# Decode step of two attention + feed-forward layers: stationary gate and up weights, group two's queries behind half of group one's scores, norm sums on the adds, value steps in other places

## The chip, the cores and the metric

The kernel runs on one core of a Trainium2 chip. The time is the device time of one execution in microseconds (us). A run more than 1.5% above the fastest run of the same kernel is marked "slow" and stays out of the ratios. A ratio is the mean time of one kernel's fast runs over that of the kernel before in the same rounds on the same chip, so it is not quite the ratio of the medians that stand beside it.

## The reference, cut to what matters

```python
x = x + attention(layernorm(x), k_cache, v_cache, wq, wo)   # layer one
x = x + ffn(layernorm(x), w_gate, w_up, w_down)
x = x + attention(layernorm(x), k_cache, v_cache, wq, wo)   # layer two: the same caches and weights
x = x + ffn(layernorm(x), w_gate, w_up, w_down)
# x: 4 x 1 x 512 bf16; 32 query heads, 8 key/value heads, 4096 positions, 128 per head
# ffn(x) = (gelu(x @ w_gate) * (x @ w_up)) @ w_down, inner width 1792
```

The two caches are 67 MB, which would be 134 MB if each layer read them. The kernel keeps a batch's keys on the chip for its second layer and loads values twice, less a few tiles that it keeps. With the weights it moves 110.4 MB.

## The kernel before

One pass per batch b: the dense part of b's first layer, then the second layer's attention of b **interleaved** with the first layer's attention of b+1. Second-layer scores read key tiles that are still on the chip; each group of four tiles is then overwritten by keys of b+1 (`keys.load`). VectorE turns every key tile once it has landed (`turn`, 1.22 us each in the mean). A **value step** is 16 matmuls on one value tile of 0.5 MB. It takes a loaded buffer, frees one, and so lets a further value load be issued. After every fourth step VectorE normalises the result. Everything is hand-scheduled. VectorE takes its work in program order in the traces: before, it sat idle for 1.84 us ahead of a normalisation at 217.47 us, and the query transpose behind that, whose rows were done at 216.92, started at 217.89. All large loads go through one queue (q1, 110.38 MB). In the trace of before, the 146 of them whose landing it tells landed in the order of their issue, tiles asked for in a row some 1.28 us apart (key tiles at 242.63, 243.91 and 245.23).

```python
def load_v():                                   # value loads; blocked while keys have the queue
    while not seen["hold"] and free and seen["load"] < seen["upto"]:
        ...
        dq.dma_start(out=v[:], in_=cache_tile(A_v_cache, b, g * GH + s, t))

def step(self, count=1):                        # a value step
    ...
    load_v()
    for i in range(CH):
        nc.tensor.matmul(self.ot[:, s % 2], lhsT=v[:, i, :], rhs=pe[:, s, c, :], ...)
    free.append(held.pop((b, g, s, t)))
    load_v()
    if self.n % (2 * NT) == 0:                  # every fourth: normalise on VectorE
        nc.vector.tensor_tensor(out=self.dst(...), in0=self.ot[:], in1=rden[:, s0:s0 + 2], op=ALU.mult)

def ffn_in(b0, nb, w_sb):                       # gate or up: activations stationary, weights moving
    for k in range(KD):
        for j in range(QD):
            nc.tensor.matmul(rows[...], lhsT=xn_bf[:, k, bs], rhs=w[:, j], ...)   # 448 columns
    return rows                                 # turned by VectorE later

def dense(b0, nb, proj, fill):
    out_proj_end(*proj)                         # T0 of the text: its first matmul
    add_y(b0, nb, y); ln_square(b0, nb)
    fill(1)                                     # fill = value steps left of the second layer
    mv = ln_center(b0, nb)
    fill(1)
    rg = ffn_in(b0, nb, wg_sb)
    sq, h = gelu(nb, rg, ln_rstd(nb, mv))       # ln_rstd: ten small VectorE operations
    fill(1)
    ru = ffn_in(b0, nb, wu_sb)
    H_bf = gate_up(nb, sq, h, ru)
    fill(3)
    y = down(nb, H_bf)
    add_y(b0, nb, y)

# between dense(b) and the next attention
    ln_square(b, 1); fill(1); mv = ln_center(b, 1); fill(1)
    rstd = ln_rstd(1, mv); am = ...             # reciprocal root of the second norm
    qr0 = q_rows(b, 1, ga); fill(1)
    qm0 = q_spread(turn_rows(qr0, 512)[:, :, 0], am, ga)
    qr1 = q_rows(b, 1, gb); fill(1)             # both groups' queries before any score
    q_build(qm0, ga); qm1 = q_spread(turn_rows(qr1, 512)[:, :, 0], am, gb)

# attend(): start of the interleaved attention
    for t in range(NT):
        scores(sc2[0], ga, t); keys.load(GH)    # four key tiles free: four loads
    last_q()                                    # q_build(qm1, gb)
    seen["hold"] = True                         # no value loads from here
    rest(2)                                     # rest = fill
    for t in range(NT):
        scores(sc2[1], gb, t); keys.load(GH)
    rest(1); seen["hold"] = False; load_v()
    p0 = soft(sc2[0]); rest(1); ...
    qm = q_spread(q1_bf[:, ga, :, b1], amask, ga)
    turn()                                      # key turn 1
    q_build(qm, ga); vals2.step(KEEP); turn(3)  # key turns 2 to 4
```

## Time and profile before

| | before |
|---|---|
| median of the runs beside the first run of the changed kernel | 324.09 us (321.3 to 324.54) |
| span of the profiled execution | 322.7 us |
| T0 of batch 0, 1, 2 and of the last pass | 135.13, 200.56, 266.49, 310.14 us |
| periods between them; T0 of the last pass to the end | 65.4, 65.9, 43.7; 12.6 us |
| value loads held up by TensorE's value steps | 70.8 us in 59 waits |
| VectorE turning keys | 75.9 us in 64 operations |

The lines that carry this are in the prediction. In all such lines the idle time in front of an instruction stands last, in square brackets, with what ended it. "x8" merges eight like instructions in a row, and the duration is then that of the whole row. L426, L446, L333, L340 and L351 are the value load, the value step, the key load, the key turn and the scores. In the changed kernel they are L446, L466, L351, L358 and L369.

### The profile page before, as it was taken

Reading aid. Unit: us, or ns where it says so; the run is one execution under the profiler, and the core shown is the slowest. Engines: PE = TensorE matmul, PEld = TensorE weight load, DVE = VectorE, ACT = ScalarE, POOL = GpSimd, SP = SyncE. Lnnn points to the kernel's source line nnn. Section 1 sums busy time; section 2 is a strip of 40 time slices with the busy share of each in tenths; the row PEclk is TensorE's granted clock in tenths of the full one; section 3 lists DMA queues with packets and bytes.
Section 4 is the critical chain, followed back from the end, with each engine's and each line's share of the span. In section 5 each row is a group of like instructions: output and inputs, shape, how many; then the busy total and the mean of one; then the engine's idle time right before and its main releaser. Section 6 shows DMA issues by size and latency. Waiting matters only on the chain.

```text
span 322.7 us, 8609 instructions
## 1 busy us (share of the span) xinstructions
PE 212.4 (66%) x3812; PEld 120.8 (37%) x3812; DVE 171.9 (53%) x459; ACT 28.9 (9%) x70; POOL 0.7 (0%) x6
## 2 busy tenths in 40 slices
PE   1460575334665369898663498989645889896864
PEld 0010244121322145663421256644202565546442
DVE  5576750033457895255497742543989435434133
ACT  0003010000020103000202021001010120012000
POOL 0000000000000000000000000000000000000000
PEclk9999999999996555556955555557655555577555
DMA  7999999999959998999899999998999999989900
GB/s 256 391 412 399 409 409 396 349 389 374 353 172 365 408 380 281 383 346 341 288 415 408 410 385 352 365 314 263 411 408 409 407 396 359 291 295 373 364 22 3
DMA packets 34646, 110.94 MB, mean 344 GB/s; under 512 B 3112, under 2 KB 9008, under 8 KB 34608
## 3 DMA queue, kind: packets, MB, share of 16 engines
q1 hardware_dynamic: 34608, 110.38, 92.0%
q8 instruction: 30, 0.49, 0.6%
q14 instruction: 8, 0.07, 0.1%
HBM read 110.37 MB, written 0.00 MB: 342 GB/s over the span
## 4 chain that ended last, share of the span: by engine, by line
DMA 57%; PE 25%; DVE 8%; SPq 6%; issue 2%; ACT 1%; ACTq 0%
DMA kt<-in_A_k_cache_dram 25%; DMA v<-in_A_v_cache_dram 23%; PE ot L446 6%; PE sc L351 6%; DMA wd_sb<-in_B_w_down_dram 5%; PE rows L209 4%; DMA kt<-in_A_v_cache_dram 3%; SPq L126 3%; DVE kt L340 2%; PE rows L264 2%; PE rows L285 2%; PE x L397 1%; PE y L270 1%; SPq L127 1%; DVE pp L378 1%
## 5 line engine op out<-in xcount | busy, mean ns | idle before, releaser
L340 DVE STREAM_TRANSPOSE kt<-kt 128x1024 f32<-128x1024 f32 x64 | 75.9, 1222 | 9.0 <-DMA kt<-in_A_k_cache_dram 8.4
L446 PEld LDWEIGHTS <-v 128*128 128x128 bf16 x1920 | 59.6, 104 | 54.9 <-DMA v<-in_A_v_cache_dram 31.0
L446 PE MATMUL ot<-pe,v 128*128 128x4 bf16 x1920 | 64.2, 166 | 23.4 <-DMA v<-in_A_v_cache_dram 19.6
L351 PE MATMUL sc<-kt,qb 128*32 128x512 bf16 x512 | 62.0, 534 | 19.3 <-DVE kt L340 16.6
L351 PEld LDWEIGHTS <-qb 128*32 128x32 bf16 x512 | 16.9, 113 | 49.5 <-issue 26.3
L199 DVE STREAM_TRANSPOSE rows<-rows 128x512 f32<-128x512 f32 (+1 forms) x25 | 17.6, 702 | 29.0 <-PE rows L264 15.3
L453 DVE TENSOR_TENSOR OT_bf<-ot,rden 128x8 bf16<-128x8 f32 x32 | 5.5, 171 | 40.4 <-PE ot L446 38.0
L370 ACT ACTIVATE pp<-sc,nm 128x512 bf16<-128x512 f32 x16 | 11.0, 688 | 158.1 <-DVE junk L366 126.8
L397 PE MATMUL x<-pp,ident_bf 128*32 128x128 bf16 x256 | 9.1, 283 | 24.1 <-DVE pp L378 23.9
L209 PE MATMUL rows<-wq_sb,xn_bf 128*1 128x512 bf16 (+1 forms) x160 | 18.6, 620 | 5.0 <-DMA wq_sb<-in_A_wq_dram 4.5
L264 PE MATMUL rows<-wo_sb,OT_bf 128*1 128x512 bf16 (+1 forms) x120 | 14.8, 614 | 6.6 <-DMA wo_sb<-in_A_wo_dram 6.4
L397 PEld LDWEIGHTS <-ident_bf 128*32 128x32 bf16 x256 | 6.7, 121 | 30.2 <-issue 28.1
L357 DVE TENSOR_REDUCE m<-sc 128x1 f32<-128x512 f32 x16 | 10.8, 673 | 12.1 <-PE sc L351 12.1
L378 DVE STREAM_TRANSPOSE pp<-pp 128x512 bf16<-128x512 bf16 x16 | 11.2, 702 | 5.6 <-ACT pp L370 5.2
L233 DVE TENSOR_TENSOR qb<-qe,amask 128x256 bf16<-128x256 f32 x16 | 6.8, 424 | 11.8 <-PE qe L230 11.8
L400 ACT CAST pe<-x 128x512 bf16<-128x512 f32 x16 | 9.4, 585 | 21.9 <-PE x L397 21.9
L315 PE MATMUL y<-H_bf,wd_sb 128*128 128x1 bf16 (+1 forms) x280 | 8.3, 165 | 3.9 <-DVE H_bf L308 2.3
L285 PE MATMUL rows<-wu_sb,xn_bf 128*1 128x448 bf16 (+1 forms) x80 | 8.4, 570 | 2.9 <-DMA wu_sb<-in_B_w_up_dram 2.9
L285 PE MATMUL rows<-wg_sb,xn_bf 128*1 128x448 bf16 (+1 forms) x80 | 8.3, 567 | 2.9 <-DMA wg_sb<-in_B_w_gate_dram 2.4
L315 PEld LDWEIGHTS <-wd_sb 128*128 128x128 bf16 x280 | 7.9, 104 | 5.6 <-DMA wd_sb<-in_B_w_down_dram 3.5
L276 DVE TENSOR_TENSOR XX<-XX,y 128x4 f32<-128x4 f32 (+1 forms) x10 | 1.6, 161 | 15.6 <-PE y L315 9.2
L383 PE MATMUL den<-zx,mean_f 128*128 128x16 f32 x32 | 8.9, 357 | 0.0
(66 smaller groups left out, 117.4 us busy)
## 6 DMA issues: line engine op xcount, KB each, us to landing
v<-in_A_v_cache_dram SPq DMA_DIRECT2D x112, 512.0 KB, 8.1
kt<-in_A_k_cache_dram SPq DMA_DIRECT2D x64, 512.0 KB, 10.6
wq_sb<-in_A_wq_dram SPq DMA_DIRECT2D x2, 2048.0 KB, 11.1
wo_sb<-in_A_wo_dram SPq DMA_DIRECT2D x4, 1024.0 KB, 12.0
kt<-in_A_v_cache_dram SPq DMA_DIRECT2D x8, 512.0 KB, 9.9
wg_sb<-in_B_w_gate_dram SPq DMA_DIRECT2D x1, 1792.0 KB, 13.4
wu_sb<-in_B_w_up_dram SPq DMA_DIRECT2D x1, 1792.0 KB
wd_sb<-in_B_w_down_dram SPq DMA_DIRECT2D x2, 896.0 KB, 16.6
```

Of the source, the lines that this page charges most:

```text
L199: nc.vector.transpose(out=rows[:, :n], in_=rows[:, :n])
L209: nc.tensor.matmul(rows[j * QS:j * QS + nb, :], lhsT=xn_bf[:, k, bs], rhs=w, start=(k == 0), stop=(k == KD - 1))
L264: nc.tensor.matmul(rows[r0:r0 + lhsT.shape[-1], :], lhsT=lhsT, rhs=wo_sb[:, i, :], start=(at == 0 and n < QD), stop=(at == 2 and n >= hp - ...
L285: nc.tensor.matmul(rows[j * QS:j * QS + nb, :KF * QS], lhsT=xn_bf[:, k, bs], rhs=w[:, j], start=(k == 0), stop=(k == KD - 1))
L315: nc.tensor.matmul(y[:, k], lhsT=wd_sb[:, c, k * P:(k + 1) * P], rhs=H_bf[:, c, :], start=(c == 0 and k == 0), stop=(c == KF - 1), skip_gr ...
L340: nc.vector.transpose(out=words, in_=words)
L351: nc.tensor.matmul(sc[s * QS:(s + 1) * QS], lhsT=qb[:, w0:w0 + 2 * W], rhs=kt[:, :, be // 2, :, be % 2], start=(t == 0 and be == 0), stop= ...
L357: nc.vector.tensor_reduce(out=m[:], in_=sc.rearrange("p c j -> p (c j)"), axis=AX.X, op=ALU.max)
L370: nc.scalar.activation(out=pp[:], in_=sc[:], func=ACT.Exp, bias=nm[:, 0:1], scale=scale, accum_out=ls[:])
L378: nc.vector.transpose(out=flat, in_=flat)
L397: nc.tensor.matmul(x[a * QS:(a + 1) * QS, s], lhsT=ident_bf[:, s * QS:(s + 1) * QS], rhs=pT[:, a], start=True, stop=True, skip_group_check ...
L446: nc.tensor.matmul(self.ot[:, s % 2], lhsT=v[:, i, :], rhs=pe[:, s, c, :], start=(c == 0), stop=(c == C - 1), skip_group_check=True)
```

## The change

The change means to bring the first key loads forward and to keep TensorE busy in its gaps. Its parts are:

- gate and up weights become the stationary operand, which spares two transposes per dense part;
- the queries of head group two are built only after half of group one's scores, whose keys are then free earlier;
- the sums for the norm come from accumulators of the adds;
- value steps move from the dense part into later gaps, and second-layer values alone may be loaded while keys have the queue.

```diff
     def ffn_in(b0, nb, w_sb):
-        for k in range(KD):
-            for j in range(QD):
-                nc.tensor.matmul(rows[...], lhsT=xn_bf[:, k, bs], rhs=w[:, j], ...)
+        for c in range(KF):
+            for k in range(KD):
+                nc.tensor.matmul(h[:, c], lhsT=w_sb[:, k, c * P:(c + 1) * P], rhs=xn_bf[:, k, bs], ...)
 ...
     def load_v():
-        while not seen["hold"] and free and seen["load"] < seen["upto"]:
-            b, g, s, t = loads[seen["load"]]
+        while free and seen["load"] < seen["upto"]:
+            b, last, g, s, t = loads[seen["load"]]
+            if seen["hold"] and not last:
+                return
 ...  attend()
-            for t in range(NT):
-                scores(sc2[0], ga, t)
-                keys.load(GH)
-            last_q()
             seen["hold"] = True
-            rest(2)
+            scores(sc2[0], ga, 0)
+            keys.load(GH)
+            qm1 = next_q()
+            scores(sc2[0], ga, 1)
+            keys.load(GH)
+            q_build(qm1, gb)
+            rest(1)
             for t in range(NT):
                 scores(sc2[1], gb, t)
                 keys.load(GH)
-            rest(1)
             seen["hold"] = False
             load_v()
             p0 = soft(sc2[0])
-            rest(1)
+            rest(2)
             soft_turn(p0)
             pe0, den0 = soft_swap(p0, p2p), soft_den(p0)
+            rest(2)
             qm = q_spread(q1_bf[:, ga, :, b1], amask, ga)
             turn()
             prob2[ga] = (pe0, soft_recip(den0))
             q_build(qm, ga)
+            rest(1)
             vals2.step(KEEP)
             turn(3)
 ...  dense()
+        fill(1)
         add_y(b0, nb, y)
         ln_square(b0, nb)
-        fill(1)
         mv = ln_center(b0, nb)
         fill(1)
         rg = ffn_in(b0, nb, wg_sb)
-        rstd = ln_rstd(nb, mv)
-        sq, h = gelu(nb, rg, rstd)
+        ru = ffn_in(b0, nb, wu_sb)
         fill(1)
-        ru = ffn_in(b0, nb, wu_sb)
-        H_bf = gate_up(nb, sq, h, ru)
-        fill(3)
-        y = down(nb, H_bf)
+        sq, h = gelu(nb, rg, ln_rstd(nb, mv))
+        y = down(nb, gate_up(nb, sq, h, ru))
+        fill(1)
 ...  between dense() and attend()
         ln_square(b, 1)
-        fill(1)
         mv = ln_center(b, 1)
         fill(1)
+        qr0 = q_rows(b, 1, ga)
+        fill(2)
         rstd = ln_rstd(1, mv)
         am = ...
-        qr0 = q_rows(b, 1, ga)
+        q_build(q_spread(turn_rows(qr0, 512)[:, :, 0], am, ga), ga)
         fill(1)
-        qm0 = q_spread(turn_rows(qr0, 512)[:, :, 0], am, ga)
-        qr1 = q_rows(b, 1, gb)
-        fill(1)
-        q_build(qm0, ga)
-        qm1 = q_spread(turn_rows(qr1, 512)[:, :, 0], am, gb)
+        def next_q():
+            return q_spread(turn_rows(q_rows(b, 1, gb), 512)[:, :, 0], am, gb)
```

The norm sums (`accum_out` on the add and on the square), the last batch's steps and one probability buffer less are left out here.

## The prediction

> **What bounds the kernel now.** I read the page first: busy shares, the DMA queue, the chain that ended last.

> ```profile
> PE 212.4 (66%) x3812; PEld 120.8 (37%) x3812; DVE 171.9 (53%) x459; ACT 28.9 (9%) x70; POOL 0.7 (0%) x6
> ...
> q1 hardware_dynamic: 34608, 110.38, 92.0%
> ...
> DMA 57%; PE 25%; DVE 8%; SPq 6%; issue 2%; ACT 1%; ACTq 0%
> ```

> No engine is near full; the DMA queue is, and the chain runs through it for 57%. At the best sustained rate in the page's slices, about 409 GB/s, 110.38 MB would take 270 us. The span is 322.7. The end holds 13.4 us without transfers (last value tile lands at 309.3), the start about 3; some 36 us are lost in between. Then the waits of the DMA queue's own engine, to see what transfers wait for:

> ```profile
> SPq L426 <- PE ot L446: 70.8, 59, 4.8
> ...
> SPq L333 <- PE sc L351: 18.3, 8, 11.5
> ```

> Value loads (L426) wait for value steps on TensorE to free a buffer, key loads (L333) for scores to free a key tile. The table by stretches shows where the rate falls:

> ```profile
> 206.00:218.00 12.00, 10.62 (x219) 6.36 (x211) 5.81 (x29) 0.22 (x1) 0.00 (x0) 0.50 0.95 324
> 218.00:224.00 6.00, 5.97 (x93) 2.73 (x97) 2.45 (x8) 0.35 (x1) 0.00 (x0) 0.65 0.86 271
> ...
> 235.00:245.00 10.00, 4.71 (x50) 2.00 (x49) 8.64 (x15) 1.67 (x4) 0.00 (x0) 0.50 1.03 410
> ```

> The last column is GB/s. The dense part and the first scores (206 to 224) run below 409; the key stretch runs full. From 200 to 226 the one-microsecond stretches miss 6.15 us of transfer. That is what the change aims at, once in each of the batch turns. The timeline of VectorE in the same turn shows the other chain, the turning of keys:

> ```profile
> 217.47 0.18 DVE L453 TENSOR_TENSOR OT_bf<-ot,rden 128x8 bf16<-128x8 f32 x1 [1.84 <-PE ot L446]
> ...
> 226.61 1.25 DVE L340 STREAM_TRANSPOSE kt<-kt 128x1024 f32<-128x1024 f32 x1 [0.16 <-DMA kt<-in_A_k_cache_dram]
> ...
> 228.62 10.16 DVE L340 STREAM_TRANSPOSE kt<-kt 128x1024 f32<-128x1024 f32 x8
> ```

> Eight turns take 10.16 us, 1.27 each, which is the landing rate of a key tile (0.524 MB at 410 GB/s is 1.28); five with tiles at hand take 5.74 (1.15 each). VectorE turns keys as they land and is nearly saturated doing so.

> [...]the normalisation of values at 217.47 sits 1.84 us for its TensorE step, and the query work behind it stays behind. [...]In the trace tiles of one queue land one after another, 1.28 us apart. [...]

> **The change part by part.** I compare the two programs' instruction order, and count time from T0, the first matmul of the closing output projection (135.13, 200.56 and 266.49; periods 65.4 and 65.9).

> *Gate and up stationary.* 16 matmuls of 448 columns (1.66 us per pass) become 56 of one column. The down projection already has that form: 56 in 1.63 to 1.67. TensorE: no change. VectorE loses two transposes of 0.66 per dense pass. In the last pass, where nothing fills, the first one stands on the chain (314.59, 0.61), and up is done before it is wanted: about -0.7 us with its gap, at the end.

> *Norm sums on the adds.* Twice per batch a reduction (0.17 + 0.03) leaves the chain, two accumulator reads of about 0.08 enter it (the row of L366 shows 0.08): -0.05 each. Nothing.

> *Dense and query chain.* After: gate and up back to back from T0+2.6 to 5.9, one step, down from 6.4 to 8.1 (before 8.1 to 9.7), mean by 9.4, query rows 9.8 to 11.7. But two value steps now stand before the reciprocal root in program order, and the first ends a head pair. Its normalisation on VectorE waits for a TensorE step that stands behind the query rows: 12.2. Only then come ten operations of 0.19 and the mask (to 14.5), transpose 0.76, spread 0.24, qe 0.25, qb 0.45: first scores at about T0+16.3. Before: 16.6, 17.5 and 17.3. [...]I give the scores the half clock (16 in 1.85): first key tiles free at about 18.0, against 17.7 in the first full period (152.86-135.13) and 19.4 in the second (219.95-200.56). So the intended lead of 4 us shrinks to -0.3 to +1.4.

> *Group two's queries after half the scores.* The second four key tiles free 1.8 + 1.8 us later, near 21.6. Four tiles in flight cover that (4 x 1.28). Scores of the second group shift from 22.0 to about 22.6.

> *Value steps moved behind the scores.* This is the part I distrust. Before, 10 of 14 remaining value steps ran ahead of the key loads, so all 14 tiles were requested first. After, 8 do. The fourteenth tile is requested by the ninth step, so in the queue it stands behind eight key tiles. Its step now stands on TensorE before the new scores, and its normalisation on VectorE between key turn 1 and key turn 2. So turns 2 to 8, which overlapped the landing of keys 2 to 8, start only after all eight keys and one value tile have landed.
> Landing: if the queue kept 1.28 per tile from tile 13 (T0+19.3): 19.3 + 9 x 1.28 = 30.8. Before, the eighth key landed 15 to 16 us after the first key's issue because the rate sags there (271 GB/s above): 18.0 + 15.5 + 1.28 = 34.8. I take 33.3. Then step and normalisation 0.7: turn 2 at 34.0, against 26.5 (161.67) and 28.1 (228.62). From turn 2 to the end of turn 16 before: 250.56-228.62 = 21.9, less 0.8 because tiles are at hand: 21.1. So turn 16 ends at 55.1, and the second half of the last scores starts there. Before it started at 51.05 and 51.6, and was held by values: the step ahead waited for its tile, with keys ready 2.4 and 1.6 us earlier. From there to the next T0 are 14.4, less 0.4 as value tiles are now at hand. Period: 55.2 + 13.9 = 69.1, so +3.7 and +3.2 us.

> *First turn (batch 0 to 1), no value steps left over:* query chain 0.25 earlier, keys landing-bound: -0.2. *Last turn:* keys are not loaded, tile 14 takes the first freed buffer, unblocked. But three steps now precede the second softmax; its probabilities reach TensorE at T0+31.9 instead of 29.3. From there 11.7 us of work (14.04 less 2.34 of waits): 43.6 against 43.4. With the tail -0.7: -0.5.

> Sum: 323.9 - 0.2 + 3.7 + 3.2 - 0.5 = 330.1. I shade it to 329.0, because someone chose this order.

> **The rivals.** (1) *Transfers stay fed, and gain wins.* If the reciprocal root ran beside the query rows and tile 14 came early, each of three turns would return up to half of its 6 us: 315. For it: the queue's 92% and its 70.8 us of waits for TensorE. Against it: the two in-order waits, which the order shows. (2) *It cancels.* With ideal landing (30.8) the turns end at 52.6: +1.2 and +0.7, total 325. For it: 2 us of slack in front of the value waits. Against it: the sag at every start of key loads. (3) *The sag is full at each start* (34.8): +5 each, 333.[...]

> **Range and chances.** The doubt is the landing of tile 14, 4 us wide and counted twice, hence 8 us between rivals 2 and 3, plus my reading of order. Range 321 to 336. Two per cent slower begins at 330.4, just above my estimate: 0.40. Two per cent faster (317.4) needs rival 1: 0.08. Between: 0.52.

> **What would show it.** Right: in the VectorE timeline of turns two and three, the first key turn, then a value normalisation with an idle time of several us ended by TensorE, that TensorE step in turn waiting for a value transfer, then seven key turns at 1.15; the value transfer issued after eight key loads; periods near 69. In the dense part ten small operations starting only after a normalisation near T0+12. In the tail no transpose, about 0.7 less. Wrong: no idle before turn 2, or tile 14 landed before T0+29, or periods under 65.

## The result, and the profile after

The changed kernel took 339.11 us (336.6 to 341.95, 4 runs, one of them slow) against 324.09 before: ratio 1.0456, 95% interval 1.0345 to 1.0568. It is slower by 4.6%, above the predicted range. The changed kernel was run once more as it stood. The lines below are from it. Its span is 340.5. The execution took 342.32 us and is the slowest of its four (median 339.77), so its periods add up to some 2 us more than is usual.

The page's busy shares, DMA queue and chain, of the changed kernel:

```profile
PE 212.5 (62%) x4212; PEld 132.0 (39%) x4212; DVE 164.8 (48%) x465; ACT 29.1 (9%) x70; POOL 0.7 (0%) x6
...
q1 hardware_dynamic: 34608, 110.38, 87.9%
...
DMA 36%; PE 31%; DVE 21%; SPq 5%; issue 4%; ACT 1%; DVEq 0%; ACTq 0%
```

TensorE is as busy as before, VectorE less by 7 us, the bytes are the same. The queue's share fell from 92.0 to 87.9%, and the chain runs through VectorE for 21% in place of 8%. Only the weight loads got more work (PEld 132.0 us in place of 120.8), and they overlap the matmuls: from 230 to 238 us 3.98 us of loads and 7.39 of matmuls lie in 8.00. The rest got later. The waits of the DMA queue's engine agree: value loads wait longer for value steps.

```profile
SPq L446 <- PE ot L466: 100.0, 59, 5.0
...
SPq L351 <- PE sc L369: 17.0, 7, 11.7
```

The periods show where. T0 lies at 135.40, 209.31, 283.14 and 328.70:

| from T0 to the next | before | predicted | after (repeat) |
|---|---|---|---|
| first turn, start to T0 of batch 0 | 135.1 | 134.9 | 135.4 |
| batch 0 to 1 | 65.4 | 69.1 | 73.9 |
| batch 1 to 2 | 65.9 | 69.1 | 73.8 |
| batch 2 to the last pass | 43.7 | 43.6 to 43.9 | 45.6 |
| last T0 to the end | 12.6 | 11.9 | 11.8 |

The third row, in the DMA queue's timeline (when loads were issued; the duration is that of issuing all of them):

```profile
229.72 5.46 SPq L351 DMA_DIRECT2D kt<-in_A_k_cache_dram  x8
236.88 0.33 SPq L446 DMA_DIRECT2D v<-in_A_v_cache_dram  x1
238.16 9.26 SPq L351 DMA_DIRECT2D kt<-in_A_k_cache_dram  x8
```

One value tile, the fourteenth of its batch, stands behind eight key tiles. Before, sixteen key loads stood in one row, with all values asked for ahead of them:

```profile
219.95 16.68 SPq L333 DMA_DIRECT2D kt<-in_A_k_cache_dram  x16
```

TensorE's and VectorE's timelines of the changed kernel show what the new order does:

```profile
247.08 1.44 PE L466 MATMUL ot<-pe,v 128*128 128x4 bf16 x48 [8.50 <-DMA v<-in_A_v_cache_dram]
```

```profile
236.96 1.23 DVE L358 STREAM_TRANSPOSE kt<-kt 128x1024 f32<-128x1024 f32 x1
...
247.71 0.18 DVE L473 TENSOR_TENSOR OT_bf<-ot,rden 128x8 bf16<-128x8 f32 x1 [8.67 <-PE ot L466]
247.79 9.12 DVE L358 STREAM_TRANSPOSE kt<-kt 128x1024 f32<-128x1024 f32 x8
```

TensorE idles 8.50 us for that tile, and VectorE 8.67 us for TensorE, between key turn 1 and key turn 2. Seven of the eight keys that it then turns stood ahead of that value tile in the queue. This is the picture that was predicted, though the idle is longer. In the stretches of this time the transfers move 276, then 413 GB/s (columns: length, busy us of PE, weight load, VectorE, ScalarE and GpSimd with their counts, granted clock, DMA share, GB/s):

```profile
230.00:238.00 8.00, 7.39 (x150) 3.98 (x143) 4.46 (x12) 1.67 (x4) 0.00 (x0) 0.84 0.85 276
238.00:247.00 9.00, 0.58 (x20) 0.41 (x17) 0.76 (x3) 0.00 (x0) 0.00 (x0) 0.57 1.03 413
```

From 238 to 247 the queue moves 413 GB/s, and VectorE works 0.76 of 9 us while key tiles that have landed stand unturned: the eight turns that then follow take 9.12 us without a wait for a transfer. What VectorE leaves undone here it has to do later in the period.

The change was to feed the transfers better. The bytes moved in the 28 us after each T0 (summed from stretches of 4 us) say that it did the reverse:

| MB in the 28 us after T0 | batch 0 | batch 1 |
|---|---|---|
| before | 9.4 | 9.0 |
| after (repeat) | 8.1 | 7.2 |

The second in-order wait is in the query chain, on VectorE:

```profile
223.86 0.18 DVE L473 TENSOR_TENSOR OT_bf<-ot,rden 128x8 bf16<-128x8 f32 x1 [2.46 <-PE ot L466]
223.94 0.15 DVE L184 TENSOR_TENSOR msq<-mv 128x1 f32<-128x1 f32 x1
...
225.87 0.23 DVE L661 TENSOR_SCALAR am<-amask,rstd 128x4 f32<-128x4 f32 x1
```

The ten operations of the reciprocal root need nothing but sums that were copied at 221.25. They start 2.7 us after that, because a value normalisation ahead of them waits for its value step, which stands behind the query rows. TensorE then waits 2.80 us for the queries, which VectorE multiplies by the mask made from that root.

A third wait was not in the prediction. TensorE's timeline in the dense part of batch 1:

```profile
219.02 0.94 PE L333 MATMUL y<-H_bf,wd_sb 128*128 128x1 bf16 x30 [2.37 <-issue]
```

"issue" is idle time in which the engine waited for nothing that the profile shows. Each dense part with value steps in it has such idles, 2.1 to 2.9 us in all. More on them below.

Three causes are thus on the table: **A**, tile 14 behind the keys; **B**, the normalisation ahead of the reciprocal root; **C**, the stationary gate and up with their idle. They can be undone one at a time.

### The profile page after: what moved, and what is told of

Its sections match the earlier page's. It is cut to its first block, busy times and chain, and to the rows that moved or that the text cites.

```text
span 340.2 us, 9425 instructions
## 1 busy us (share of the span) xinstructions
PE 212.3 (62%) x4212; PEld 132.2 (39%) x4212; DVE 164.8 (48%) x465; ACT 29.2 (9%) x70; POOL 0.7 (0%) x6
## 2 busy tenths in 40 slices
DMA packets 34649, 110.99 MB, mean 326 GB/s; under 512 B 3112, under 2 KB 9008, under 8 KB 34608
## 3 DMA queue, kind: packets, MB, share of 16 engines
q1 hardware_dynamic: 34608, 110.38, 88.0%
## 4 chain that ended last, share of the span: by engine, by line
DMA 38%; PE 28%; DVE 21%; SPq 6%; issue 5%; ACT 1%; DVEq 0%; ACTq 0%
DMA v<-in_A_v_cache_dram 17%; DMA kt<-in_A_k_cache_dram 13%; DVE kt L358 11%; PE sc L369 7%; PE ot L466 6%; DMA wd_sb<-in_B_w_down_dram 5%; DMA kt<-in_A_v_cache_dram 3%; PE rows L224 3%; PE rows L304 3%; SPq L127 3%; PE y L333 2%; PE rows L279 2%; PE x L415 1%; DVE rows L214 1%; DVE m L375 1%
## 5 line engine op out<-in xcount | busy, mean ns | idle before, releaser
L466 PE MATMUL ot<-pe,v 128*128 128x4 bf16 x1904 | 63.1, 166 | 35.3 <-DMA v<-in_A_v_cache_dram 24.0
L358 DVE STREAM_TRANSPOSE kt<-kt 128x1024 f32<-128x1024 f32 x64 | 74.6, 1214 | 4.5 <-DMA kt<-in_A_k_cache_dram 4.4
L369 PE MATMUL sc<-kt,qb 128*32 128x512 bf16 x512 | 64.8, 543 | 15.7 <-DVE kt L358 12.8
L369 PEld LDWEIGHTS <-qb 128*32 128x32 bf16 x512 | 17.4, 114 | 47.3 <-issue 28.5
L214 DVE STREAM_TRANSPOSE rows<-rows 128x512 f32<-128x512 f32 x15 | 10.9, 730 | 34.8 <-PE rows L224 19.5
L375 DVE TENSOR_REDUCE m<-sc 128x1 f32<-128x512 f32 x16 | 10.9, 678 | 12.5 <-PE sc L369 12.5
L245 PE MATMUL qe<-qm,t_bf 128*128 128x64 bf16 x16 | 3.4, 213 | 14.9 <-DVE qm L235 14.1
L333 PE MATMUL y<-H_bf,wd_sb 128*128 128x1 bf16 (+1 forms) x280 | 8.5, 165 | 4.4 <-DMA wd_sb<-in_B_w_down_dram 2.7
L304 PE MATMUL rows<-xn_bf,wg_sb 128*128 128x1 bf16 (+1 forms) x280 | 8.3, 165 | 3.9 <-DMA wg_sb<-in_B_w_gate_dram 2.4
L304 PE MATMUL rows<-xn_bf,wu_sb 128*128 128x1 bf16 (+1 forms) x280 | 8.3, 165 | 3.7 <-DMA wu_sb<-in_B_w_up_dram 2.9
L292 DVE SCALAR_TENSOR_TENSOR XX<-XX,y 128x4 f32<-128x4 f32 x8 | 1.3, 158 | 18.9 <-PE y L333 13.6
L333 PEld LDWEIGHTS <-wd_sb 128*128 128x128 bf16 x280 | 8.1, 104 | 4.7 <-DMA wd_sb<-in_B_w_down_dram 2.9
L304 PEld LDWEIGHTS <-wg_sb 128*128 128x128 bf16 x280 | 8.2, 105 | 4.1 <-DMA wg_sb<-in_B_w_gate_dram 2.5
## 6 DMA issues: line engine op xcount, KB each, us to landing
wo_sb<-in_A_wo_dram SPq DMA_DIRECT2D x4, 1024.0 KB, 11.9
wd_sb<-in_B_w_down_dram SPq DMA_DIRECT2D x2, 896.0 KB, 16.8
```

Of the source, the lines that this page charges most:

```text
L214: nc.vector.transpose(out=rows[:, :n], in_=rows[:, :n])
L304: nc.tensor.matmul(h[:, c], lhsT=w_sb[:, k, c * P:(c + 1) * P], rhs=xn_bf[:, k, bs], start=(c == 0 and k == 0), stop=(k == KD - 1), skip_g ...
L333: nc.tensor.matmul(y[:, k], lhsT=wd_sb[:, c, k * P:(k + 1) * P], rhs=H_bf[:, c, :], start=(c == 0 and k == 0), stop=(c == KF - 1), skip_gr ...
L358: nc.vector.transpose(out=words, in_=words)
L369: nc.tensor.matmul(sc[s * QS:(s + 1) * QS], lhsT=qb[:, w0:w0 + 2 * W], rhs=kt[:, :, be // 2, :, be % 2], start=(t == 0 and be == 0), stop= ...
L375: nc.vector.tensor_reduce(out=m[:], in_=sc.rearrange("p c j -> p (c j)"), axis=AX.X, op=ALU.max)
```

## The experiments

All outputs are right. "Base" names the kernel that the diff is against.

**1. The changed kernel again** (4 runs).

> The changed kernel once more, for a profile in the fast state and an interval. Every theory expects 336 to 341 us and a period from one closing output projection to the next of about 73 us in the second and third batch (before: 65.4 and 65.9), with the value step before the new scores waiting about 8 us for its tile.

339.77 us, ratio 1.0492 (1.0427 to 1.0558). The result stands, and this run's profile is the one read above.

**2. A undone: one value step more ahead of the scores** (base: after).

```diff
         q_build(q_spread(turn_rows(qr0, 512)[:, :, 0], am, ga), ga)
-        fill(1)
+        fill(2)
 ...  attend(), attend_last()
         q_build(qm1, gb)
-        rest(1)
```

> The changed kernel with one value step moved from behind group two's queries to ahead of the first scores, so that the fourteenth value tile is requested before the eight keys instead of behind them. Theory A (that tile's wait holds VectorE between key turn 1 and 2): the wait of 8 us is gone in both periods, turn 8 ends some 7 us earlier, the value waits behind it take some of it back, periods near 67, time 325 to 329. Rival D (the key loads themselves come slowly because they now come in two bursts of four): the wait only changes its name, keys land as late, periods stay above 71, time 336 to 340.

328.44 us, ratio 1.0136 (1.007 to 1.0202): 11 of the 15 us come back. Periods are 66.0 and 67.3. The queue's timeline, then VectorE's, then TensorE's:

```profile
221.92 15.63 SPq L351 DMA_DIRECT2D kt<-in_A_k_cache_dram  x16
```

```profile
228.99 1.23 DVE L358 STREAM_TRANSPOSE kt<-kt 128x1024 f32<-128x1024 f32 x1
...
231.03 0.18 DVE L473 TENSOR_TENSOR OT_bf<-ot,rden 128x8 bf16<-128x8 f32 x1
231.11 9.12 DVE L358 STREAM_TRANSPOSE kt<-kt 128x1024 f32<-128x1024 f32 x8
```

```profile
249.06 0.59 PE L466 MATMUL ot<-pe,v 128*128 128x4 bf16 x16 [3.02 <-DMA v<-in_A_v_cache_dram]
```

All sixteen keys are asked for in one row. The normalisation waits for nothing, and eight turns run in 9.12 us right behind turn 1. In their place waits for value tiles return later in the period, 3.02 us here, so not all of the 8.67 us are gained. Rival D is out: the keys still come in two bursts of four, and the periods are well under 71.

**3. B undone: the reciprocal root ahead of the two value steps** (base: after).

```diff
         qr0 = q_rows(b, 1, ga)
-        fill(2)
         rstd = ln_rstd(1, mv)
         am = ...
+        fill(2)
```

> The changed kernel with the reciprocal root placed ahead of the two value steps in program order. Theory B (the normalisation in between makes the root wait for the query rows): first scores 2 us earlier in all three later batches; as the landing of tile 14 follows the first key request, both periods and the last batch shorten by about 2, time 332 to 335. If only A counts and the keys' landing is bound by transfers that are late anyway: under 1 us in all.

331.94 us, ratio 1.0235 (1.0182 to 1.0287). VectorE's timeline:

```profile
219.06 0.16 DVE L184 TENSOR_TENSOR msq<-mv 128x1 f32<-128x1 f32 x1
...
221.48 0.17 DVE L473 TENSOR_TENSOR OT_bf<-ot,rden 128x8 bf16<-128x8 f32 x1 [0.26 <-PE ot L466]
221.56 0.72 DVE L214 STREAM_TRANSPOSE rows<-rows 128x512 f32<-128x512 f32 x1
```

The ten operations follow the sums at once, and the normalisation waits 0.26 in place of 2.46. The periods are 70.9, 71.0 and 42.0, some 3 us shorter each than in the repeat, where 2 were expected.

**4. C undone: gate and up moving again** (base: after; `ffn_in`, `gelu` and `gate_up` of before).

> The changed kernel with gate and up computed as before (activations stationary, weights moving, 16 matmuls each, with the two transposes on VectorE). Theory C (with 56 pairs each, TensorE runs through its instructions faster than they are fetched, and stands idle 2.2 to 2.7 us per dense part with no wait on any engine): the unexplained idle of TensorE in the dense part is gone, two transposes of 0.66 are back and cost about 1.2, so each later batch gains 1.0 to 1.5, the tail loses 0.7: 335 to 337, 2 to 4 us under the changed kernel of these rounds. If the idle has another cause, it stays and the transposes cost: 341 to 343.

339.14 us, ratio 1.0466 (1.0415 to 1.0517), against 1.0492 for the changed kernel: 0.3%, within the intervals. That lies in neither of the two ranges that were expected. TensorE's timeline from the down projection of batch 1 on:

```profile
214.44 1.65 PE L335 MATMUL y<-H_bf,wd_sb 128*128 128x1 bf16 x56 [0.71 <-DVE H_bf L328]
215.95 0.57 PE L468 MATMUL ot<-pe,v 128*128 128x4 bf16 x16
```

The one idle, of 0.71 us, is for VectorE's product and not "issue". From 115 us on this run has one "issue" idle of 0.29 us on TensorE, in the last turn, and the kernel before has none. So the idles of the dense parts belong to the stationary form. In time, what they cost is, within the intervals, what the two transposes of 0.66 us cost that come back here. VectorE's timeline of this run, from the same turn, serves further down:

```profile
220.00 0.18 DVE L475 TENSOR_TENSOR OT_bf<-ot,rden 128x8 bf16<-128x8 f32 x1 [2.46 <-PE ot L468]
...
244.28 0.18 DVE L475 TENSOR_TENSOR OT_bf<-ot,rden 128x8 bf16<-128x8 f32 x1 [8.84 <-PE ot L468]
```

**5. A and B undone** (base: after).

> Both mended: fourteenth tile ahead of the keys, reciprocal root ahead of the value steps. tile14_first alone came to 1.014 of the kernel before and norm_early to 1.024 where the changed kernel has 1.049. If the two losses are separate and simply add (theories A and B), 1.014 less 0.025 is 0.99, 320 to 323 us. If they are two ways to the same loss (an earlier first score also brings tile 14 earlier, so norm_early bought part of A's wait), about 1.00 to 1.01, 324 to 328; then value transfers bound both, as they bound the kernel before.

322.92 us in 20 runs, ratio 0.9984 (0.9957 to 1.0011). Parity: A and B carry the whole loss. The time lies in the range expected if the two add, the ratio between the two expectations.

**6. A, B and C undone** (base: after).

> As tile14_norm, and gate and up with moving weights again. What is left of the change then: the split of the queries, the norm sums, fewer value steps ahead of the keys. Theory C (instruction fetch): TensorE's idle without a wait in the dense part goes, the transposes return, 1 us or so per later batch won, tail 0.5 to 0.7 lost: 0 to 3 us under tile14_norm. If transfers bound the periods by then, no difference but the tail, 0 to 1 us slower.

321.53 us (20 runs, three of them slow), ratio 0.9973 (0.9942 to 1.0004).

**7. Only the stationary gate and up** (base: before).

> The kernel before with gate and up stationary and nothing else of the change. Theory C: TensorE's idle without a wait appears here too, 1 to 3 us per dense part, at distances of 128 pairs; against it four transposes of 0.66 leave two chains, and the tail is 0.5 to 0.8 shorter: 322 to 326, no clear difference. If the idle came from the new order of steps instead, there is none here, and each dense part is over 1 us shorter: 319 to 322.

324.19 us, ratio 1.0002 (0.9961 to 1.0043). Its end is 0.8 us shorter (11.7), and it has 4.3 us of "issue" idle on TensorE in the dense parts, which eats what the transposes had cost there.

**8. Only the split of group two's queries** (base: before).

```diff
-            for t in range(NT):
-                scores(sc2[0], ga, t)
-                keys.load(GH)
-            last_q()
+            scores(sc2[0], ga, 0)
+            keys.load(GH)
+            qm1 = last_q()                    # rows, transpose and spread of group two
+            scores(sc2[0], ga, 1)
+            keys.load(GH)
+            q_build(qm1, gb)
```

> The kernel before with the second group's query rows between the two halves of the first scores, and nothing else. Theory A and B say the split itself is harmless: first keys requested 1.9 us earlier, the second four 1.8 later than they would be then, 322 to 325. Rival D (two bursts of four keys starve the queue, so the split costs): 327 or more, with a dip in the rate between the bursts.

320.79 us, ratio 0.9887 (0.9779 to 0.9995), with one of four runs slow: a gain, outside both expectations, but with too wide an interval.

**9. All three undone, A put back.**

> From all_three (0.997 of the kernel before), with only one step undone: one value step back behind group two's queries, so tile 14 is again requested behind eight keys. This is cause A alone. Theory A: the wait of 8 to 9 us returns, both periods grow from 64.7 to about 69 to 71 us, time 329 to 333. If A hurts only together with a late first score (B and C), the growth is under 2 us per period: 322 to 326.

331.30 us, ratio 1.0234 (1.0165 to 1.0303). Periods are 69.1 and 69.3, what the prediction had for the whole change.

**10. All three undone, B put back.**

> From all_three, with only the two value steps back ahead of the reciprocal root. Cause B alone. The first scores come about 2 us later in each of three batches; value transfers hide part of it in the two full periods, nothing hides it in the last batch: 324 to 328. If transfers hide it wholly in the full periods: 322 to 324.

327.55 us, ratio 1.0105 (1.0041 to 1.0169). With this the table of all eight combinations is full (each run against before on its own chip; three chips in all):

| | B absent | B present |
|---|---|---|
| A absent, C absent | 0.9973 | 1.0105 |
| A absent, C present | 0.9984 | 1.0136 |
| A present, C absent | 1.0234 | 1.0466 |
| A present, C present | 1.0235 | 1.0492 |

A costs 2.5 to 2.6% where B is absent and 3.6% where it is present. B costs 1.3 to 1.5% without A and 2.3 to 2.6% with it. C costs 0.0 to 0.3%. The interplay of 1% is no larger than its uncertainty: put together from the intervals, that of either half of the table is about 1.1%. A possible reason is that B makes the first key load late, and with A tile 14 stands behind those keys, so that the delay is passed on to all turns; this is not shown.

**11. The split alone again** (5 rounds).

> before_split once more with five rounds, as its first interval was 0.978 to 1.000. If the split alone gains (first keys requested earlier in three batches, 1 us each), 0.985 to 0.993; if the three fast runs were a lucky draw, 0.995 to 1.005.

319.49 us, ratio 0.9828 (0.9766 to 0.9891). Two of its six runs were slow and are left out, as are four of the 25 of before on that chip. The medians of all runs give 319.49 over 323.40, that is 0.988. The gain is clear of the noise, and lies near 1.1 to 1.7%.

**12. All three undone, the steps behind the query spread** (base: 6; two steps move behind the spread, and the last batch's second softmax ahead of its three steps).

> all_three with two more moves of the same kind: the two value steps go behind the query spread in program order, so no normalisation stands before the transpose of the query rows, and in the last batch the second softmax is put ahead of the three value steps. If the last waits of VectorE for value steps still count: 0.3 to 0.8 us per batch and 1 us in the last, 318 to 320.5, under 0.992 of the kernel before. If value transfers bound the full periods, only the last batch shortens: 320 to 321.5.

322.38 us (20 runs, two of them slow), ratio 0.997 (0.9944 to 0.9997). Nothing gained over run 6. A miss.

After this one question was open: run 6 contains the split, and yet gains 0.3% where the split alone gains 1.1 to 1.7%.

**13. The split and the norm sums** (base: before; the first-pass probabilities have one buffer only, as in the change).

> The kernel before with the split of group two's queries and also the norm sums on the adds (first-pass probabilities in one buffer instead of two[...]). Theory S (the norm sums, or the single buffer that pays for them, cost the 1.4% between the split alone, 0.983, and all three parts undone, 0.997): 0.993 to 1.000, about 322 to 324 us. Rival R (they are free, the loss is in how many value steps stand ahead of the keys): 0.980 to 0.988, about 319 us.

321.77 us, ratio 0.9882 (0.9828 to 0.9935), half of its six runs slow. The medians of all runs, 321.77 over 323.42, give 0.995, so the ratio leans on which runs count as slow.

**14. All three undone, value steps placed in the dense part as before** (base: 6; some lines joined).

```diff
-        fill(1)
         add_y(b0, nb, y); ln_square(b0, nb)
+        fill(1)
         mv = ln_center(b0, nb); fill(1)
         rg = ffn_in(b0, nb, wg_sb)
+        sq, h = gelu(nb, rg, ln_rstd(nb, mv)); fill(1)
         ru = ffn_in(b0, nb, wu_sb)
-        fill(1); sq, h = gelu(nb, rg, ln_rstd(nb, mv))
-        y = down(nb, gate_up(nb, sq, h, ru)); fill(1)
+        H_bf = gate_up(nb, sq, h, ru); fill(3)
+        y = down(nb, H_bf)
 ...  between dense() and attend(), behind ln_center
-        fill(1)
 ...  attend(), behind q_build(qm, ga)
-            rest(1)
 ...  attend_last()
-        rest(3)
+        rest(2)
```

> All three parts undone, and the steps of the dense part placed as in the kernel before, so that ten value steps stand ahead of the keys instead of nine and three of them fill the wait for the down projection. Rival R (the placing of the value steps is what is left of the loss): 0.980 to 0.988, about 319 us. Theory S (norm sums or their buffer): unchanged, 0.994 to 1.000.

321.69 us (one of six runs slow), ratio 0.9927 (0.9872 to 0.9982). Both runs fall between the theories. By its fast runs the kernel with the sums lands outside what theory S expected, with all runs inside it, so the sums are not shown to cost anything, nor to be free. The placing reaches part of the way that rival R expected. The intervals of 13, 14 and 6 overlap, so what separates run 6 from the split alone stays open.

**15. The split, and gate and up stationary in the last pass only** (base: 8), where no value steps run.

```diff
+        if nb == 1:                            # as before: moving, turned by VectorE
+            ...
+        else:                                  # the last pass, four batches at once
+            rg, ru = ffn_still(b0, nb, wg_sb), ffn_still(b0, nb, wu_sb)
+            sq, h = gelu(nb, rg, ln_rstd(nb, mv))
```

> The kernel before with the split of group two's queries, and gate and up stationary in the last pass alone, where no value steps run[...]. If the end's gain of 0.76 us stands by itself and the idle for instructions needs the crowded dense parts: 0.5 to 0.9 us below the split alone, so 0.980 to 0.985, about 318.5 us, with the last out-projection to the end 11.8 us instead of 12.6. If the stationary form costs TensorE as much there too: the same as the split alone and an end of 12.5.

319.88 us, ratio 0.9869 (0.982 to 0.9918), two of six runs slow. In its profile (span 315.3, the shortest of all) the last T0 to the end is 11.7 us, as expected. The ratio lies just outside the expectation, and cannot tell 0.8 us from the split alone. The bytes moved do not settle where the split gains:

| MB in the 28 us after T0 | batch 0 | batch 1 |
|---|---|---|
| before | 9.4 | 9.0 |
| the split alone (run 11, slow profile) | 9.3 | 9.2 |
| run 6, which contains the split | 9.2 | 9.3 |
| run 15 | 10.0 | 10.4 |

In run 15 the slices of 4 us from T0+16 to T0+28 move 406, 312, 394 and 404, 356, 411 GB/s, where before moved 325, 233, 405 and 355, 211, 342. But up to the last pass TensorE runs the same instructions in runs 11 and 15, and the profile of run 11 has the sag: 362, 238, 380 and 367, 267, 384. Run 6 moves no more bytes than before either. So one execution alone suggests that keys freed earlier fill the sag, and where the split gains is not shown. The split alone and this version beat both kernels, with ratios to before between 0.983 and 0.989 in three runs (8, 11 and 15).

## Why the prediction was wrong, point by point

The direction, the two waits in program order (2.46 and 8.67 us on VectorE in the turn shown above) and their places were right. The size was not: +8.5 and +7.9 us per full turn instead of +3.7 and +3.2. Two terms of the sum were too small: the landing of tile 14 (15.3 us from the first key load, measured 16.8 and 17.4) and TensorE's time for gate and up ("no change", measured 1.6 and 2.4 us late). Each term, from T0, with the two full turns of the repeat:

| step | predicted | measured, batch 0 | batch 1 |
|---|---|---|---|
| normalisation ahead of the reciprocal root | 12.2 | 13.8 | 14.6 |
| first scores | 16.3 | 17.7 | 18.5 |
| first key load issued | 18.0 | 19.6 | 20.4 |
| tile 14's step starts | 33.3 | 36.4 | 37.8 |
| key turn 2 | 34.0 | 37.1 | 38.5 |
| end of key turn 16 | 55.1 | 58.2 | 59.5 |
| next T0 | 69.1 | 73.9 | 73.8 |

Of the 4.8 and 4.7 us by which the turns were longer than predicted, 1.6 and 2.4 were there at the first line of this table, 1.5 and 2.1 came with the landing of tile 14, and 1.8 and 0.3 behind key turn 16.

**"Gate and up stationary ... TensorE: no change" failed.** The query chain was 1.6 and 2.4 us late before it reached the first in-order wait. In run 4, with gate and up moving, it is there at T0+12.1 and 12.6, as predicted. The idle that makes the difference stands in front of a gate matmul, a down projection or a value step with "issue" as its reason: 2.17 us in batch 0, 0.52 and 2.37 in batch 1. The stationary form has two times 56 pairs of matmul and weight load per pass in place of two times 16, which is 160 instructions more in the same few us. Two idles of one dense part (they end at 213.09 and 219.02) are exactly 128 pairs apart (30 + 56 + 16 + 26), which is 256 instructions. The raw transfer records have, on an instruction queue, packets of 16,384 bytes:

```text
repeat of the changed kernel, queue 8, packets of 16,384 bytes: start, us (each took 1.0 to 1.1)
140.81   210.49   216.68   285.63   290.64
TensorE leaves an "issue" idle at
143.32   213.09   219.02   287.99   293.09
```

Each idle ends 2.3 to 2.6 us after such a packet starts. In run 15 two idles of 1.65 and 1.50 us, in a row of value steps in its last turn (289.27 and 295.62), end 2.2 and 2.4 us after packets at 287.04 and 293.22. So it is not bound to gate and up; value steps in a long row had it too.

**"I take 33.3" for the landing of tile 14 was between two estimates, and the worse one held.** This is the step that failed in any case, for run 4, with its query chain as predicted, took 339.14 us as well. From the first key load to tile 14's step took 16.8 us and 17.4 us; the working allowed 15.3, and rival 3, the sag in full, had 16.8. The sag is there: 276 GB/s from 230 to 238 at a DMA share of 0.85, as the 271 at 0.86 before; what causes it is not shown. Run 4 shows the two errors apart. There A and B are present without C's idle: the key loads start at T0+17.9 and 18.4 (18.0 predicted), but tile 14's step comes 17.0 and 17.8 us later, key turn 2 at 35.6 and 37.0, and the periods are 71.0 and 72.4. Run 9 has the predicted period, 69.1 and 69.3, by luck alone: without B the key loads start at T0+16.2 and 16.4, and the landing takes its 17 us, so that key turn 2 comes at 33.7 and 33.9, near the 34.0 that the working had for A and B together.

**B was seen and its cost was followed only halfway.** The working had the wait at T0+12.2 and the first key load at 18.0. Of its two estimates of the landing, 34.8 starts from that key load; 30.8 starts from tile 13 and does not contain it, and the working took a value between. Measured by itself, in the table of eight, B costs 1.3 to 1.5%, some 4 to 5 us over three turns, which is about what the split gains by itself. With A it costs 2.3 to 2.6%.

**The rest of the period was as predicted, with a remainder.** From key turn 2 to the end of turn 16: 21.1 in both turns, predicted 21.1. From there to the next T0: 15.8 and 14.3, predicted 14.0 (the working writes 55.2 + 13.9 where its own terms are 55.1 and 14.0; the sum is the same); the waits for value tiles that were to vanish did not quite (0.29 and 0.69 us in batch 0).

**The last turn** was to gain its waits as well: 11.7 us from the second probabilities to T0. They reached TensorE at T0+31.3 (31.9 predicted), but T0 came 14.3 us later, which is what before took: the working put that at 14.04 and the period before at 43.4, and the trace has 14.31 and 43.65. So this turn too was longer than predicted, 45.6 for 43.6 to 43.9. TensorE's timeline:

```profile
317.74 0.59 PE L466 MATMUL ot<-pe,kt 128*128 128x4 bf16 x16 [0.46 <-DMA kt<-in_A_v_cache_dram]
319.01 0.59 PE L466 MATMUL ot<-pe,kt 128*128 128x4 bf16 x16 [0.69 <-DMA kt<-in_A_v_cache_dram]
...
327.85 0.59 PE L466 MATMUL ot<-pe,v 128*128 128x4 bf16 x16 [0.65 <-DMA v<-in_A_v_cache_dram]
```

These steps wait for transfers, and three steps placed earlier did not bring the tiles earlier.

**The tail** was right: 11.8 us instead of 12.6, with VectorE going straight from the root to the gate. Before and after:

```profile
314.53 0.67 DVE L199 STREAM_TRANSPOSE rows<-rows 128x448 f32<-128x448 f32 x1
```

```profile
333.00 0.16 DVE L199 SCALAR_TENSOR_TENSOR rstd<-r,rstd 128x4 f32<-128x4 f32 x1
333.26 0.22 DVE L311 TENSOR_TENSOR h<-rows,rstd 128x56 f32<-128x56 f32 x1
```

**The split** was rightly seen as cheap (shifting the second group by 0.6 us). What it is worth by itself, 1.1 to 1.7%, the working did not take apart from the rest. **The norm sums** are not shown to cost or gain anything. **The shade** from 330.1 to 329.0 "because someone chose this order" went the wrong way: it was no reading of the profile.

Of the rivals, the third (sag in full, 333) came nearest, and it too lacked the late key load. The granted clock of the dense part of batch 1 was 0.50 before (206 to 218 us) and stayed at 0.50 (209 to 221 us). The first named what would have had to be different: the root beside the query rows and tile 14 early. Run 5 is that kernel. It gives back 5%, but ends at parity and not at 315, since waits for value tiles return.

## What to carry to other kernels

Before moving fill-in work on an in-order engine, ask of each piece what it waits for and who stands behind it: one value tile asked for eight key tiles too late held VectorE for 8.7 us with its own work at hand. A delay ahead of a shared queue belongs in every estimate of what queues behind it: here the first key load came at T0+19.6 and 20.4 us for 18.0, and the step of tile 14, behind the keys, 16.8 and 17.4 us after it. And when large matmuls become many small ones, count instructions as well as busy time: 160 more per dense part came with 2.1 to 2.9 us of "issue" idle here.
